# A four-batch retention and low-rank mixer kernel: batches 1 to 3 in natural token order, stored by whole tiles

## The chip, the cores and the metric

The kernel runs on one core of a Trainium2 chip. A time is the device time of one execution in microseconds, given as the median of several executions. Line numbers (L757 and so on) are those of the kernel before.

## What is computed

There are 4 batches, 8 heads, 768 tokens and a head width of 64. The first half is a linear recurrence per head, the second a mixer over tokens and then over channels; everything comes in and goes out as fp32.

```python
# q, k, v: [4, 8, 768, 64]; gamma[h] = 1 - 2**(-5-h)
for t in range(768):
    state = gamma * state + outer(k[:, :, t], v[:, :, t])
    y[:, :, t] = q[:, :, t] @ state / 8
x = y moved to [4, 768, 512]           # heads side by side
h = x.transpose(0, 2, 1) @ U @ V       # over tokens, rank 32: U [768, 32], V [32, 768]
u = x + h.transpose(0, 2, 1)
out = u + relu(u @ w_ch1) @ w_ch2      # over channels, 512 -> 2048 -> 512
```

## The kernel before, in words

**Stages.** The recurrence is done in blocks of tokens: a score matrix inside a block (L505), a causal mask on it (L511, `mask`), the product with v (L527) and, for what came before the block, a running state (L489, L522). Batch 0 has functions of its own (`turn_block`, `score_block`, `mix_block`). For batches 1 to 3, `weave` (L820) interleaves the recurrence of batch b with the channel mixer of batch b-1: the mixer's pieces (`mlp_pieces`, L746) stand in a fixed order, and each step of the recurrence has a written-out place, a share of the pieces' total cost. Each engine works through its own instructions in the order in which they were written down.

**The mixer of a batch.** `up` (L757) makes gT = relu(w1 u): 16 pieces over the first four blocks of 128 tokens (`lo`), 16 over the last two (`hi`), woven as eight `lo`, eight `hi`, and then the rest. The relu is done by ScalarE (L764), for every fourth piece by VectorE (L762), and frees one of four PSUM banks. It reads uT, the transposed u, which for batches 2 and 3 comes from three DMA transposes on SyncE's queue (`lr_turn`, L591); the third holds the last two token blocks and so serves the `hi` pieces. `down` (L805, batch 0) and `down_pairs` (batches 1 to 3) make the second product; `down_pairs` uses a scheme with 7 products in place of 8 (L649, sums in L599). `give` (L670) and `halves` (L710) finish an output tile of 128 tokens and put it on the list `stores`.

**Token order.** q arrives two neighbouring tokens to a partition, each a run of 128 numbers ("(p two)"), so that a descriptor is 512 bytes long. After the transpose, `q_order` (L452) copies the two halves into place: for block x, first the even tokens, then the odd ones ("two m"). Hence x, u and the output tiles have even tokens in partitions 0 to 63 and odd ones in 64 to 127; U and V are brought into that order at the start (`spread_u`, `spread_v`), `mask` is made from `t2` (the same order), and `store` (L603) writes every tile as two DMAs of 64 partitions, one to the even and one to the odd rows.

**Queues.** SyncE issues all loads (`feed_one`, L155), the transposes of k and q of batches 2 and 3 (`turn_dma`, L474), those of u (L591) and most stores (L608). Loads go through a ring of 16 tiles: GpSimd takes one (`prep_keys`, L304 and L306; `prep_w1`, `prep_w2`) and the next load follows. The stores of batch 1 are issued by ScalarE (12 DMAs), those of batches 0, 2 and 3 by SyncE, except one of the last. In the program as built, every DMA takes the next of eight completion semaphores in program order and, before it is issued, waits for the DMA that used it last, so DMA n waits for DMA n-8 whatever queue that is on. GpSimd also makes half of the sums of w2 (L599, `w2_sums`).

Of the kernel before, what the change touches and what calls it, by code (L numbers as in the profile page):

```python
# [13 lines left out]
ALU = mybir.AluOpType  # L14
# [4 lines left out]
def kernel(  # L19
# [63 lines left out]
    def evac(eng, dst, src):  # L83
        if eng == "A":
            nc.scalar.activation(dst, src, AF.Copy)  # L85
        else:
            nc.vector.tensor_copy(out=dst, in_=src)
# [5 lines left out]

    Ub = wts.tile([P, NCK, RK], fp16)
    V4 = wts.tile([P, S], fp16)
    VR = NSC * RK
    Uf = blk.tile([P, NSC, 2, RK], fp32, bufs=1)
    Vf = blk.tile([VR, SC], fp32, bufs=1)  # L100
# [36 lines left out]
    def feed_one(hold=True):  # L137
        if n_fed[0] == len(feed):
            return
        if hold and feed[n_fed[0]][0][:2] == ("k", 3):  # L140
            return
        key, src = feed[n_fed[0]]
        n_fed[0] += 1
        if key[0] == "uv":
            nc.sync.dma_start(
                out=Uf.rearrange("p s two r -> p s (two r)"),
                in_=moe_U.rearrange("(s p two) r -> p s (two r)", p=P, two=2))
            nc.sync.dma_start(
                out=Vf, in_=moe_V.rearrange("r (f t) -> (r f) t", f=NSC))
            return  # L150
        t = rin.tile([P, 512], fp32, tag="in", name=f"in_{n_fed[0]}")
        ready[key] = t
        if key[0] in "qkv":
            t = t.rearrange("p (h d) -> p h d", h=H if len(key) == 3 else 4)
        nc.sync.dma_start(out=t, in_=src)  # L155

# [14 lines left out]
    for b in range(1, B):  # L171
        for sc in range(NSC):
            feed_keys(pair(b, sc)[AHEAD * (b == 1 and sc == 0):])
    for _ in range(RING):
        feed_one()

# [23 lines left out]
    def tables(eng, dims, iota, only_k=False):  # L200

        n = len(dims)
        lg = consts.tile([P, *dims, H], fp32, name=f"lg{n}")
        pos = consts.tile([P, *dims, H], fp32, name=f"pos{n}")
        t = [consts.tile([P, *dims, H], fp32, name=f"g{i}{n}")
             for i in ("kk" if only_k else "qk")[only_k:]]
        nc.gpsimd.iota(pos, base=0, allow_small_or_imprecise_dtypes=True, **iota)
        for h in range(H):
            eng.memset(lg[..., h], gammas_log[h])
        eng.tensor_tensor(pos, pos, lg, op=ALU.mult)  # L210
        nc.scalar.activation(t[-1], pos, AF.Exp, scale=-1.0)
        if only_k:
            return t[0]
        nc.scalar.activation(t[0], pos, AF.Exp)
        eng.tensor_scalar(t[0], t[0], 1.0 / math.sqrt(D), None, op0=ALU.mult)
        return t
# [108 lines left out]
        return u_p  # L325

    def hold_u(u_p):
        evac("A", Ub.rearrange("p (s x) r -> p x s r", x=2),
             u_p[:, :NCK * RK].rearrange("p (x s r) -> p x s r", x=2, s=NSC))

    def spread_v():
        v_p = [bank(t) for t in ("st", "qk")]
        for f in range(NSC):
            nc.tensor.matmul(v_p[f // 2][:, ts(f % 2, SC)], v_sel[:VR, f], Vh,
                             start=(f % 2 == 0), stop=True,
                             skip_group_check=True)
        evac("A", V4[:, :2 * SC], v_p[0])
        evac("A", V4[:, 2 * SC:], v_p[1][:, :SC])

    def prep_w1(mb):  # L340
        for c in range(NCB):
# [109 lines left out]

    def q_order(b, sc, src):  # L452
        t = rmid.tile([P, 2, 4, P], bf16, tag="qO", bufs=2, name=f"qO_{b}_{sc}")
        dst = t.rearrange("p x n (two m) -> p two n x m", two=2)
        src = src.rearrange("p two n (x m) -> p two n x m", x=2)
        for two in range(2):
            evac("A" if b == 1 else "D", dst[:, two], src[:, two])
        live["qO", b, sc] = t
# [82 lines left out]
    def lr_proj(b):  # L541
        p_p = bank("o" if b else "s")
        for j in range(NCK):
            for c in range(NCB):
                nc.tensor.matmul(p_p[ds(RK * c, RK), :P], Ub[:, j],
                                 xs[b][:, j, ts(c, P)], start=(j == 0),
                                 stop=(j == NCK - 1))
        pcs[b] = rmid.tile([P, P], fp16, tag="pc", name=f"pc_{b}")
        evac("D", pcs[b], p_p[:, :P])
# [3 lines left out]
    def lr_grow(b, j0, nj, last="qk"):  # L553
        banks = [bank(t) for t in ("s", "s", "o", last)]
        grown[b] = banks
        for j in range(j0, j0 + nj):
            for c in range(NCB):
                nc.tensor.matmul(banks[c][:, ts(j - j0, P)],
                                 V4[ds(RK * c, RK), ts(j, P)],
                                 pcs[b][ds(RK * c, RK)], start=True, stop=True)  # L560

    def lr_add(b, j0, nj, cs=range(NCB)):
# [40 lines left out]
    def store():  # L603
        if stores:
            eng, dst, src = stores.pop(0)
            dst = dst.rearrange("(p two) c -> two p c", two=2)
            for i in range(2):
                eng.dma_start(out=dst[i], in_=src[ds(HP * i, HP)])  # L608

    def chain(*fs):  # L610
        def f():
# [134 lines left out]
    def mlp_pieces(b):  # L746
# [52 lines left out]
        def down(j, m0):  # L799
            def f():  # L800
                if m0 == 0:
                    hold[j] = bank("mlp")
                ch = hold[j]
                for m in range(m0, m0 + 4):
                    nc.tensor.matmul(ch, gT[:, m, ts(j, P)], w2b[:, m],  # L805
                                     start=(m == 0), stop=(m == NM - 1))
                if m0 == NM - 4:
                    o_sb = outp.tile([P, DM], fp32, tag="o_sb",
                                     name=f"o_{b}_{j}")
                    nc.vector.tensor_tensor(o_sb, ch, us[b][:, j], op=ALU.add)  # L810
                    stores.append((nc.scalar if b else nc.sync,
                                   out[b, ts(j, P)], o_sb))
            return f

        for j in range(NCK):
# [41 lines left out]
    for sc in range(NSC):  # L857
        last = sc + 1 == NSC
        keep_busy(3 if sc else 9, fresh=not last, wide=not sc)
        turn_block("k", sc, "D")  # L860
        keep_busy(0 if sc else 7, wide=True)
        turn_block("q", sc, "AD" if last else "A")
        prep_pair("v", sc, "PD" if last else "PA")
        if sc:
            state_half(sc - 1, 1)
        else:
            keep_busy(4)
        score_block(sc, 0)
        if last:
            prep_uv()  # L870
        else:
            prep_pair("k", sc + 1, "PD")
            prep_block("P", "q", sc + 1, 0)
            keep_busy(0 if sc else 3)
        if sc:
            score_block(sc, 1, "mlp", "DA")
        else:
            score_block(sc, 1)
        if last:
            u_p = spread_u()  # L880
            state_half(sc, 0)
            hold_u(u_p)
            mix_block(sc - 1, "AD")
            continue
        prep_block("D", "q", sc + 1, 1)
        if sc:
            mix_block(sc - 1, "AA")
        keep_busy(4 if sc else 1, fresh=sc > 0)
        state_half(sc, 0)
        if sc == 0:  # L890
            nc.vector.tensor_scalar(mask, t2.rearrange("p two m -> p (two m)"),
                                    srange, None, op0=ALU.is_ge)
    for mb in range(4):
        prep_w1(mb)
    mix_block(NSC - 1, "AD", ("s", "s"))
# [11 lines left out]
    idle_bank[0] = bank("s")  # L907
    for c in range(NCB):
        nc.tensor.matmul(xT[c][:, :LO], pcs[0][ds(RK * c, RK)],
                         V4[ds(RK * c, RK), :LO], start=False, stop=True,  # L910
                         skip_group_check=True)
    for c in range(NCB):
        evac("AD"[c % 2], uTs[0][:, :NLO, c], four(xT[c]))
# [7 lines left out]
    for b in range(1, B + 1):  # L921
# [10 lines left out]
        if b < B:  # L932
            if b == 1:
                at = [0.475, 0.575, 0.63, 0.69, 0.745, 0.8]
                lag = [0.01, 0.035, 0.065]
                for sc in range(NSC):
                    keys = pair(b, sc)
                    c0, c1 = 2 * sc, 2 * sc + 1
                    if sc:
                        tracks.append(([part(prep_keys, b, keys[:AHEAD])],  # L940
                                       at[c0] - 0.1, 1))
                    tracks.append(([part(prep_keys, b, keys[AHEAD:])],
                                   at[c1] - 0.1, 1))
                    for f, d in ((part(turn_pe, "q", b, sc),
                                  at[c0] - (0.035, 0.025, 0.03)[sc]),
                                 (part(turn_pe, "k", b, sc, (0,)), at[c0]),
                                 (part(turn_pe, "k", b, sc, (1,)), at[c1])):
                        tracks.append(([f], d, d))
                for sc in range(NSC):
                    tracks.append(([part(prep_keys, 2, pair(2, sc))],  # L950
                                   at[-1] - 0.05 + 0.03 * sc, 1))
# [83 lines left out]
```

## Time and profile before

| | |
|---|---|
| median of 5 runs | 227.77 us (226.03 to 229.68) |
| the profiled execution | 227.15 us, of which the span shown is 225.3 us |
| granted TensorE clock | 9 of 10 or more in every slice |
| TensorE busy (PE) | 213.2 us, 95% |
| VectorE (DVE), ScalarE (ACT), GpSimd (POOL) busy | 143.6, 89.2 and 92.3 us |
| packets on SyncE's DMA queue | 83776, 36.84 MB |
| stores, SyncE's queue | 32 of 128 KB, 6 of 64 KB, 2 of 32 KB |
| stores, ScalarE's queue | 12 of 128 KB, 2 of 32 KB |

PE, DVE, ACT, POOL are engines; SPq and ACTq are the instruction queues of SyncE and ScalarE, where DMAs are issued. A row of the timeline is: start, duration, engine, line, operation, out<-in, and in brackets how long the engine stood idle before it and what ended that. A row of the groups has busy time, mean ns of one and idle time before them. The chain of waits follows the work that ended last backwards to what released it. The whole profile is of one execution.

### The profile page before, as it was taken

How to read it: one execution, taken by the hardware profiler on the slowest of the kernel's cores; microseconds unless marked ns; L12 is line 12 of the kernel's file. 1: busy time of each engine (PE TensorE's matmuls, PEld its weight loads, DVE VectorE, ACT ScalarE, POOL GpSimd, SP SyncE). 2: the span in 40 equal slices, each digit the busy share in tenths (PEclk: the TensorE clock that was granted, in tenths of full speed). 3: DMA queues.
4: the chain of work that ended last, by engine and by line, in shares of the span. 5: the costliest groups of instructions: out<-in, count | busy, mean ns of one | idle time of the engine just before them, and what ended most of it. 6: DMA issues, size and time to landing. Idle time of an engine off the chain costs nothing.

```text
span 225.3 us, 5543 instructions
## 1 busy us (share of the span) xinstructions
PE 213.2 (95%) x2235; PEld 148.0 (66%) x2235; DVE 143.6 (64%) x294; ACT 89.2 (40%) x187; POOL 92.3 (41%) x129
## 2 busy tenths in 40 slices
PE   7898999999999999899999995999999999999991
PEld 2677844695565455665887852755888847668891
DVE  6488546336585572999896653596967543766541
ACT  3266654474664136576410006667310036550000
POOL 5467878887788789910599400000000000000000
PEclk9999999999999999999999999999999999999999
DMA  6999999999989999999999999000002990000263
GB/s 178 300 293 267 285 370 290 370 319 219 233 179 252 230 245 190 197 206 235 223 219 230 191 249 206 4 0 3 0 3 65 153 203 1 3 1 0 54 146 83
DMA packets 84921, 38.83 MB, mean 172 GB/s; under 512 B 58816, under 2 KB 77984, under 8 KB 84896
## 3 DMA queue, kind: packets, MB, share of 16 engines
q1 hardware_dynamic: 83776, 36.84, 70.0%
q10 hardware_dynamic: 1120, 1.64, 2.6%
q8 instruction: 17, 0.28, 0.6%
q14 instruction: 8, 0.07, 0.1%
HBM read 27.46 MB, written 6.29 MB: 150 GB/s over the span
## 4 chain that ended last, share of the span: by engine, by line
PE 70%; DVE 8%; SPq 8%; DMA 7%; issue 3%; POOL 1%; ACT 0%; ACTq 0%; POOLq 0%; DVEq 0%
PE mlp L757 33%; PE A L649 9%; PE mlp L805 9%; SPq L155 4%; PE C L649 3%; DMA in<-in_q_dram 3%; SPq L591 3%; DMA qT<-qd 3%; PE B L649 2%; DVE gS L599 2%; PE s L505 2%; DVE a L511 2%; PE o L527 2%; DMA uT<-x 1%; PE qk L464 1%
## 5 line engine op out<-in xcount | busy, mean ns | idle before, releaser
L757 PE MATMUL mlp<-uT,w1b 128*128 128x512 f16 (+1 forms) x512 | 88.8, 326 | 3.0 <-ACT gT L764 2.4
L764 ACT ACTIVATE gT<-mlp 128x512 f16<-128x512 f32 (+1 forms) x94 | 45.2, 490 | 65.9 <-PE mlp L757 45.4
L757 PEld LDWEIGHTS <-w1b 128*128 128x128 f16 x512 | 48.4, 98 | 33.9 <-issue 3.4
L762 DVE TENSOR_SCALAR gT<-mlp 128x512 f16<-128x512 f32 (+1 forms) x34 | 18.9, 555 | 30.5 <-PE mlp L757 30.5
L649 PEld LDWEIGHTS <-gT 128*128 128x128 f16 x288 | 27.5, 98 | 3.5
L511 DVE TENSOR_TENSOR a<-s,mask 128x512 bf16<-128x512 f32 x36 | 23.1, 683 | 9.8 <-PE s L505 9.6
L805 PE MATMUL mlp<-w2b,gT 128*128 128x512 f16 x96 | 24.1, 380 | 0.0
L306 POOL TENSOR_TENSOR kd<-in,gk 128x512 bf16<-128x512 f32 x18 | 19.2, 1076 | 5.6 <-DMA in<-in_k_dram 5.5
L649 PEld LDWEIGHTS <-gS 128*128 128x128 f16 x200 | 19.3, 98 | 2.6
L85 ACT ACTIVATE x<-o 128x512 f16<-128x512 f32 x20 | 11.9, 596 | 21.1 <-PE o L527 20.9
L306 POOL TENSOR_TENSOR qd<-in,gq 128x512 bf16<-128x512 f32 x18 | 19.1, 1078 | 1.4 <-DMA in<-in_q_dram 1.4
L649 PE MATMUL A<-w2t,gT 128*128 128x256 f16 x144 | 18.3, 273 | 0.0
L85 ACT ACTIVATE state<-st 64x256 bf16<-64x256 f32 x40 | 15.0, 375 | 5.4 <-PE st L385 3.9
L805 PEld LDWEIGHTS <-gT 128*128 128x128 f16 x96 | 8.2, 98 | 7.5
L304 POOL CAST vd<-in 128x512 bf16<-128x512 f32 x18 | 11.5, 650 | 1.4 <-PE s L505 0.7
L342 POOL CAST w1b<-in 128x512 f16<-128x512 f32 x16 | 9.6, 614 | 2.3 <-DMA in<-in_moe_w_ch_dram 1.8
L348 POOL CAST w2b<-in 128x512 f16<-128x512 f32 x16 | 9.6, 614 | 1.5 <-DMA in<-in_moe_w_ch_dram 1.0
L564 DVE TENSOR_TENSOR x<-s,x 128x256 f16<-128x256 f32 (+1 forms) x16 | 8.1, 551 | 2.1 <-ACT gT L764 1.1
L649 PE MATMUL B<-w2b,gT 128*128 128x256 f16 x72 | 9.4, 273 | 0.0
L649 PE MATMUL A<-w2t,gS 128*128 128x256 f16 x72 | 9.2, 273 | 0.0
L649 PE MATMUL A<-w2b,gT 128*128 128x256 f16 x72 | 9.0, 273 | 0.0
L599 DVE TENSOR_TENSOR gS<-gS,gT 128x768 f16<-128x768 f16 x12 | 8.3, 690 | 0.3
(148 smaller groups left out, 280.6 us busy)
## 6 DMA issues: line engine op xcount, KB each, us to landing
in<-in_moe_w_ch_dram SPq DMA_DIRECT2D x32, 256.0 KB, 5.7
in<-in_k_dram SPq DMA_DIRECT2D x24, 256.0 KB, 5.4
in<-in_q_dram SPq DMA_DIRECT2D x24, 256.0 KB, 5.1
in<-in_v_dram SPq DMA_DIRECT2D x24, 256.0 KB, 5.5
out_dram<-o SPq DMA_DIRECT2D x32, 128.0 KB, 2.4
out_dram<-o ACTq DMA_DIRECT2D x12, 128.0 KB, 4.1
out_dram<-o SPq DMA_DIRECT2D x6, 64.0 KB, 2.1
Uf<-in_moe_U_dram SPq DMA_DIRECT2D x1, 96.0 KB, 6.0
```

The costliest lines, as they stand in the source:

```text
L85: nc.scalar.activation(dst, src, AF.Copy)
L304: nc.gpsimd.tensor_copy(out=t, in_=src)
L306: nc.gpsimd.tensor_tensor(t, src, g, op=ALU.mult)
L342: nc.gpsimd.tensor_copy(out=w1b[:, c, ts(mb, 512)], in_=take("w1", mb, c))
L348: nc.gpsimd.tensor_copy(out=w2b[:, m], in_=take("w2", m))
L511: nc.vector.tensor_tensor(a, four(sp[i]), causal(mask), op=ALU.mult)
L599: return lambda: f(*args, **kw)
L649: nc.tensor.matmul(acc[key, i], lhs[:, m, ts(i, P)], rhs[:, m], start=(fresh and m == 0), stop=(m == NH - 1), skip_group_check=True)
L757: nc.tensor.matmul(g_p[:, :sz], w1b[:, c, ts(m, P)], uTs[b][:, ds(j, nj), c], start=(c == 0), stop=(c == NCB - 1))
L762: nc.vector.tensor_relu(gT[:, m, ds(lo, sz)], g_p[:, :sz])
L764: nc.scalar.activation(gT[:, m, ds(lo, sz)], g_p[:, :sz], AF.Relu)
L805: nc.tensor.matmul(ch, gT[:, m, ts(j, P)], w2b[:, m], start=(m == 0), stop=(m == NM - 1))
```

## The change

`q_order` writes the two halves interleaved ("m two": every second element) and not one after the other, so from there on batches 1 to 3 are in natural token order; batch 0 stays as it was. Batches 1 to 3 therefore have U and V of their own (`Ub[1]`, `V4[1]`): a new step `order_uv` loads U once more through the ring of 16, ahead of batch 2's keys, in runs of 128 bytes, and GpSimd casts it and copies V4 into natural order (two GpSimd instructions, one DMA). It stands at the share `at[-1] - 0.06` of batch 1's weave, just ahead of `prep_keys` for batch 2. `mask` is made from `jmat`. `store` issues one DMA for a tile; batch 0's tiles are put on the list as two halves, as before. So batch 1 has 6 stores on ScalarE's queue in place of 12; batches 2 and 3 have half as many on both queues. Two small tables move to a pool that is released earlier.

```diff
-    Ub = wts.tile([P, NCK, RK], fp16)
-    V4 = wts.tile([P, S], fp16)
+    Ub = [wts.tile([P, NCK, RK], fp16, name=f"Ub{i}") for i in range(2)]
+    V4 = [wts.tile([P, S], fp16, name=f"V4{i}") for i in range(2)]
...
+        if b == 1:
+            feed.append((("u",), moe_U.rearrange("(j p) r -> p j r", p=P)))
...
+    def order_uv():
+        nc.gpsimd.tensor_copy(
+            out=Ub[1], in_=take("u")[:, :NCK * RK].rearrange(
+                "p (j r) -> p j r", j=NCK))
+        feed_one()
+        nc.gpsimd.tensor_copy(
+            out=V4[1].rearrange("p (j t two) -> p j two t", two=2, t=HP),
+            in_=V4[0].rearrange("p (j two t) -> p j two t", two=2, t=HP))
...
     def q_order(b, sc, src):
         t = rmid.tile([P, 2, 4, P], bf16, tag="qO", bufs=2, name=f"qO_{b}_{sc}")
-        dst = t.rearrange("p x n (two m) -> p two n x m", two=2)
+        dst = t.rearrange("p x n (m two) -> p two n x m", two=2)
...
-                nc.tensor.matmul(p_p[ds(RK * c, RK), :P], Ub[:, j],
+                nc.tensor.matmul(p_p[ds(RK * c, RK), :P], Ub[b > 0][:, j],
...
-                                 V4[ds(RK * c, RK), ts(j, P)],
+                                 V4[b > 0][ds(RK * c, RK), ts(j, P)],
...
     def store():
         if stores:
             eng, dst, src = stores.pop(0)
-            dst = dst.rearrange("(p two) c -> two p c", two=2)
-            for i in range(2):
-                eng.dma_start(out=dst[i], in_=src[ds(HP * i, HP)])
+            eng.dma_start(out=dst, in_=src)
...
-                    stores.append((nc.scalar if b else nc.sync,
-                                   out[b, ts(j, P)], o_sb))
+                    dst = out[b, ts(j, P)].rearrange("(p two) c -> two p c",
+                                                     two=2)
+                    for i in range(2):
+                        stores.append((nc.sync, dst[i], o_sb[ds(HP * i, HP)]))
...
-            nc.vector.tensor_scalar(mask, t2.rearrange("p two m -> p (two m)"),
-                                    srange, None, op0=ALU.is_ge)
+            nc.vector.tensor_scalar(mask, jmat, srange, None, op0=ALU.is_ge)
...
+                tracks.append(([order_uv], at[-1] - 0.06, 1))
```

More of the change, by code (lines that the diff above doesn't have):

```diff
@@ L152, in feed_one @@
         ready[key] = t
-        if key[0] in "qkv":
+        if key[0] == "u":
+            t = t[:, :NCK * RK].rearrange("p (j r) -> p j r", j=NCK)
+        elif key[0] in "qkv":
             t = t.rearrange("p (h d) -> p h d", h=H if len(key) == 3 else 4)
@@ L202, in tables @@
         n = len(dims)
-        lg = consts.tile([P, *dims, H], fp32, name=f"lg{n}")
-        pos = consts.tile([P, *dims, H], fp32, name=f"pos{n}")
+        lg = blk.tile([P, *dims, H], fp32, name=f"lg{n}", bufs=1)
+        pos = blk.tile([P, *dims, H], fp32, name=f"pos{n}", bufs=1)
         t = [consts.tile([P, *dims, H], fp32, name=f"g{i}{n}")
@@ L327, in hold_u @@
     def hold_u(u_p):
-        evac("A", Ub.rearrange("p (s x) r -> p x s r", x=2),
+        evac("A", Ub[0].rearrange("p (s x) r -> p x s r", x=2),
              u_p[:, :NCK * RK].rearrange("p (x s r) -> p x s r", x=2, s=NSC))
@@ L336, in spread_v @@
                              skip_group_check=True)
-        evac("A", V4[:, :2 * SC], v_p[0])
-        evac("A", V4[:, 2 * SC:], v_p[1][:, :SC])
+        evac("A", V4[0][:, :2 * SC], v_p[0])
+        evac("A", V4[0][:, 2 * SC:], v_p[1][:, :SC])
+    def order_uv():
[6 more added lines that the diff above has]
+            in_=V4[0].rearrange("p (j two t) -> p j two t", two=2, t=HP))
     def prep_w1(mb):
@@ L909 @@
         nc.tensor.matmul(xT[c][:, :LO], pcs[0][ds(RK * c, RK)],
-                         V4[ds(RK * c, RK), :LO], start=False, stop=True,
+                         V4[0][ds(RK * c, RK), :LO], start=False, stop=True,
                          skip_group_check=True)
```

## The prediction

> **What bounds the kernel now.** I read the engine shares first, then the chain of waits, then the timeline around each place where TensorE (PE) waits.
>
> ```profile
> PE 213.2 (95%) x2235; PEld 148.0 (66%) x2235; DVE 143.6 (64%) x294; ACT 89.2 (40%) x187; POOL 92.3 (41%) x129
> ```
>
> PE is busy for 95% of the span. The change adds and removes no matmul, so only PE's gaps and what follows its last matmul can move. From 28 us on the timeline has five gaps: 0.68 at 92.3, 0.31 at 100.7, 0.28 at 113.9, 2.41 at 135.3 and 0.55 at 180.8; then 4.3 us from PE's last product (about 221.0 with its sum) to the end. The chain of waits goes through the largest gap:
>
> ```profile
> 123.74 1.29 DVE x L564 x2
> ...
> 129.16 1.44 SPq L474
> ...
> 130.69 5.75 DMA qT<-qd
> ...
> 136.47 0.47 ACTq L608
> ...
> 137.06 0.61 ACT gT L764
> ...
> 137.71 1.02 PE mlp L757 x4
> ```
>
> ScalarE's last store of batch 1 waits for a transpose of q (landing 136.45); behind it on ScalarE stand the relus of batch 2's mixer, and behind those PE, for want of a free bank. The timeline there, and at the next gap:
>
> ```profile
> 121.67 15.27 ACTq L608 DMA_DIRECT2D out_dram<-o  x12
> ...
> 136.87 1.68 SPq L591 DMA_TRANSPOSE uT<-x  x1
> 137.06 1.57 ACT L764 ACTIVATE gT<-mlp 128x512 f16<-128x512 f32 x3 [18.43 <-DMA out_dram<-o]
> 137.71 1.02 PE L757 MATMUL mlp<-uT,w1b 128*128 128x512 f16 x4 [2.41 <-ACT gT L764]
> ...
> 142.05 1.47 PE L757 MATMUL mlp<-uT,w1b 128*128 128x256 f16 x12
> ```
>
> ```profile
> 171.69 3.71 SPq L608 DMA_DIRECT2D out_dram<-o  x6
> ...
> 175.56 3.91 SPq L591 DMA_TRANSPOSE uT<-x  x2
> ...
> 181.37 8.81 PE L757 MATMUL mlp<-uT,w1b 128*128 128x512 f16 x48 [0.55 <-DMA uT<-x]
> ```
>
> Six stores stand ahead of batch 3's transposes of u on SyncE, and PE waits 0.55 us for the second.
>
> **The change, part by part.**
>
> *Place A, ScalarE's stores of batch 1 (12 to 6).* The wait of each store follows from the count of semaphores: transfer n waits for n-8. Before, the last two waited for kT and qT of batch 3's middle block. Counted again with half the stores, the six wait for: a load, a load, a load, qT of batch 3's first block, the first uT, and a store issued at 125.4. These land at about 120.2, 121.1, 122.8, 129.1 (issued 122.5, 6.5 to landing), 130.6 and 130.4. The last store now waits for its own data: VectorE's row L670 at 131.34 plus 0.42 is 131.76. An issue costs 0.55 us here, so ScalarE is free at about 132.4, when PE's first bank of batch 2 (131.46 plus 0.98) is ready, in place of 137.06. The 2.41 us go.
>
> What is late next: the `hi` pieces. PE starts them at 142.05, 4.34 us after the gap's end at 137.71; without the gap at 139.64. They read the third uT, issued at 136.87 and 3.7 us from issue to landing: 140.6. Left as it is, it puts back 0.95 us. Two things move it. (a) SyncE issues kT, qT and that uT back to back at 1.93, 1.98 and 1.68 us while ScalarE's stores run; where no store runs (91.3, 178.2, 183.4) one takes 1.3. With those stores done by 134.5 it could be up to 1.3 us sooner, 139.3. (b) `order_uv` adds a load to the same stream (below), up to 0.7 us later, 141.3. The DMA engines' share is 0.94 from 131 to 142, and the stores keep their bytes. [...] I take 140.3, nearer to the rule: **A gives 1.75 us** (0.75 to 2.41).
>
> *Place B, batch 2's stores (6 issues ahead of uT to 3).* Their last data come from L670 at 173.44 plus 0.42, 173.86; one issue of 0.55 brings SyncE to uT at 174.5 in place of 175.56. Both transposes (3.91) and 3.1 to land give 180.3 or sooner, and PE is ready at 180.82. **B gives 0.55 us** (0.4 to 0.55). The third uT comes earlier too; PE needs it only after eight pieces.
>
> *Place C, the end.*
>
> ```profile
> 211.55 11.41 SPq L608 DMA_DIRECT2D out_dram<-o  x16
> ...
> 220.74 0.29 DVE L710 TENSOR_TENSOR o<-B,db 128x128 f32<-128x128 f32 x1 [0.16 <-PE B L705]
> ```
>
> The last sum ends at 221.03. SyncE is then still issuing second halves: its two DMAs for this piece start at 221.8 and 222.4, and the latter lands 1.9 later, at 224.3. After: one store of o_3_5 from 220.3 to 220.85, then the last from 221.05, landing 2.1 later (the median of stores of 64 KB) at 223.15. **C gives 1.2 us** (0.9 to 1.35).
>
> *The copies of q_order on VectorE* (6 in batch 2, 6 in batch 3) now write every second element. The groups by form:
>
> ```profile
> L87 DVE COPY qO<-qT 128x512 bf16<-128x512 bf16 x12 | 4.8, 445 | 0.0
> L272 DVE CAST v<-in 128x512 bf16<-128x512 f32 x1 | 0.4, 427 | 0.0
> L762 DVE TENSOR_SCALAR gT<-mlp 128x512 f16<-128x512 f32 x17 | 11.7, 690 | 21.5 <-PE mlp L757 21.5
> ```
>
> A free copy takes 284 to 288 ns (minimum and median in the tile's view; the first two, held by something, 1.24 us at most). [...] The first two pairs lie on the chain (89.96 to 101); the third and batch 3's have slack (PE has no gap from 137.7 to 180.8). Cost 0.55 (0.3 to 2.4).
>
> *order_uv.* GpSimd: casts of 192 and 512 elements take 342 and 614 ns, so U's is 0.34 and V's, 768 elements, 0.83 by the same slope (up to 1.3 if its stride costs): 1.2 us. The load: 768 runs of 128 bytes. By bytes (98 of 262 KB) it is 0.37, by runs (768 of 1024) 0.75 of a load of k, which follow each other at about 1.35 us: 0.5 to 1.0, I take 0.7. PE needs Ub[1] at 75.96 and V4[1] at 77.39; the load takes the place of one that landed at 67.4, so both are there by 69. Everything behind it on SyncE and GpSimd slides: batch 2's loads, its six transposes, batch 0's stores (from 92.66), batch 3's loads (from 100.3), and the w2 sums (87.0). The first reader to notice is VectorE:
>
> ```profile
> 85.13 1.25 SPq L474 DMA_TRANSPOSE qT<-qd  x1
> ...
> 90.57 2.39 DVE L87 COPY qO<-qT 128x512 bf16<-128x512 bf16 x2
> ...
> 93.01 0.40 PE L505 MATMUL s<-qO,kT 64*128 64x128 bf16 x8 [0.68 <-DVE qO L87]
> ```
>
> That qT lands 4.4 after its issue, at 89.5, and is wanted at 90.6: a cover of 1.0 against 0.7. If the cover is gone, relus and sums queue behind the copy on VectorE and PE waits for them; 0 to 0.3. The w2 sums are wanted only at 112.5, 16 us after they end. Batch 3's slide meets a SyncE pause of 0.8 us at 124.3 and ends there, except in the transfers (term b of A).
>
> *The sum.* Batch 2's costs (0.55, with qT 0.7) come before A. They make PE reach `hi` at 140.2 to 140.35, when the third uT is there at 140.3 anyway: they cost nothing more, their cover being that wait. ScalarE's own q_order copies (594 ns, batch 1) have no row with such a stride; at double they add 1.2 us a pair, ScalarE is about 55% busy there and PE has no gap; a gain is excluded, none is my value, 0.6 the upper end. The mask, the tables and natural order as such cost nothing: same instructions, sizes and order. So 1.75 + 0.55 + 1.2 = 3.5: the span goes from 225.3 to 221.8, the profiled execution from 227.15 to 223.65. The median shown is 0.62 above that execution: **224.3 us**.
>
> **The rivals.**
> - *Nothing takes the place of the stall.* The third uT comes by 139.6 and batch 2's costs hide: 2.41 + 0.55 + 1.2 = 4.2, 223.6. For it: the 1.3 us issues where no store runs. Against it: a DMA share near 1.
> - *The transfers take it back,* or the change does not free ScalarE: uT at 141.3 or later, or another late semaphore. A gives 0.3: 2.0 in all, 225.8. For it: same bytes and one more load. Against it: the waits as counted.
> - *Slower: batch 2's stage on VectorE becomes the bound.* From 90 to 118 VectorE is busy for over 90%. While GpSimd makes the w2 sums (87.04 to 96.58) VectorE's copies take 1.24 for 0.29 and its sums 1.06 to 1.42 for 0.55. If GpSimd's sums slide by 3 us, into the second pair of copies and the sums after 97, that is two copies at 0.95 and six sums at 0.5 to 0.87, some 6 us. B and C return 1.75 and A at most 2.41, so it decides from 4.2 us of PE delay on; at 6, 229.5. Against it: the slide is worked out at 1.2, not 3.
>
> **How the numbers follow.** The forecast has 0.55, the full gain 0.15, the transfers 0.20, the slower one 0.10. One per cent is 2.3 us, about what a measurement of this kernel can tell from no change. Below 225.5: most of the forecast (0.49), the full gain (0.14), a little of the third (0.04): 0.67. Above 230.0: 0.06. Between: 0.27. The likeliest case alone has 223.5 to 225.7 by the ends of A, B and C; with the runs' scatter and the third rival, 222.8 to 226.6 holds 8 in 10.
>
> **What would show it.** Right: ScalarE's relus of batch 2 start within 1 us of PE's first piece; PE's wait of 2.41 is gone, and a wait for uT of 0 to 1 us stands ahead of `hi`; none for uT at batch 3's start; last store issued within 0.1 us of the last sum; copies of q_order at 0.43; GpSimd's two new instructions 1.2 together. Wrong: ScalarE still waiting for a transpose, copies at 0.69, VectorE waiting for qT at 91, or PE gaps from 90 to 118 above 2 us.

## The result, and the profile after

| | before | changed |
|---|---|---|
| median of all runs | 227.77 us (223.96 to 230.49, 80 runs) | 225.83 us (223.78 to 229.22, 43 runs) |
| ratio, first measurement | | 0.9965 (95%: 0.9944 to 0.9985) |
| ratio, again on another chip | | 0.9927 (0.9892 to 0.9962) |
| the profiled execution, its span | 227.15, 225.3 us | 225.9, 224.1 us |

The ratios leave out each kernel's slowest runs (over 1.5% above its fastest), which are more frequent in the kernel before, so that the medians lie further apart, 1.9 us, than the ratios say. By the two ratios the change is worth 0.8 and 1.7 us, where 3.5 were forecast. The time itself lies in the range given; the forecast gain is two to four times the one measured.

These are the lines that answer to those of before. First the busy time of the engines:

```profile
PE 214.6 (96%) x2235; PEld 148.1 (66%) x2235; DVE 143.5 (64%) x294; ACT 90.3 (40%) x187; POOL 93.9 (42%) x131
```

The two added GpSimd instructions are there (131 for 129). The chain of waits through batch 2's first mixer pieces (start, duration, what):

```profile
128.00 1.23 SPq L604
...
129.33 5.38 DMA uT<-x
...
134.85 2.75 PE mlp L768 x12
...
139.89 3.25 DMA uT<-x
...
143.18 1.48 PE mlp L768 x12
```

ScalarE's stores have gone from the chain, and transposes of u stand in their place. The timeline at the same place:

```profile
124.50 10.54 ACTq L619 DMA_DIRECT2D out_dram<-o  x6
...
134.85 2.75 PE L768 MATMUL mlp<-uT,w1b 128*128 128x512 f16 x12 [0.49 <-DMA uT<-x]
...
135.99 0.60 ACT L775 ACTIVATE gT<-mlp 128x512 f16<-128x512 f32 x1 [14.53 <-DMA out_dram<-o]
...
139.89 1.28 SPq L604 DMA_TRANSPOSE uT<-x  x1
...
143.18 1.48 PE L768 MATMUL mlp<-uT,w1b 128*128 128x256 f16 x12 [0.15 <-DMA uT<-x]
```

ScalarE's first relu starts 1.14 us after TensorE's first product (before: 5.6). The wait of 2.41 us is gone, but TensorE waits 0.49 and 0.15 for the second and third uT, and it comes to this place at 134.85, not at 131.46. The timeline at batch 3's start and at the end:

```profile
172.83 2.85 SPq L619 DMA_DIRECT2D out_dram<-o  x3
175.86 3.61 SPq L604 DMA_TRANSPOSE uT<-x  x2
...
212.09 9.85 SPq L619 DMA_DIRECT2D out_dram<-o  x8
...
221.28 0.29 DVE L721 TENSOR_TENSOR o<-B,db 128x128 f32<-128x128 f32 x1 [0.15 <-PE B L716]
```

At batch 3's start (181 before) TensorE has no wait any more, and from its last product to the end pass 2.9 us in place of 4.6. The groups by form, and VectorE's copies in the tile's view (minimum, median, maximum):

```profile
L87 DVE COPY qO<-qT 128x512 bf16<-128x512 bf16 x12 | 5.9, 550 | 0.0
...
L85 ACT ACTIVATE qO<-qk 128x512 bf16<-128x512 bf16 x6 | 4.0, 740 | 2.1 <-PE qk L477 2.1
...
L349 POOL COPY V<-V 128x768 f16<-128x768 f16 x1 | 1.0, 1049 | 0.0
...
L345 POOL CAST Ub<-in 128x192 f16<-128x192 f32 x1 | 0.3, 347 | 0.0
```

```profile
L87 DVE COPY qO<-qT x12: 447/450/1393, 92.7 to 157.1; 128x512 bf16<-128x512 bf16 x12
```

A free strided copy on VectorE takes 447 to 450 ns (284 to 288 before), on ScalarE 740 (594).

**Where it went, by the two traces.** The matmuls are the same 2235 in the same order, so the start of one in both traces gives TensorE's lateness, after minus before, at a time of the trace before. It is 0.7 us at 52, 2.10 from 70 to 89, 2.83 at 109 and still 2.83 at 131. Across place A it falls to 1.14, at batch 3's start to 0.54, and the end comes 1.2 sooner. So A gave 1.69, B 0.60 and C 1.75, in all 4.0 where 3.5 were forecast, and 2.83 had been lost ahead of A, where the forecast let 0.7 be lost and hidden. (How much of the 2.83 is the change's, and how much is the scatter of single executions, the experiments tell.)

### The profile page after: what moved, and what is told of

It is laid out like the page before. It is cut to its first block, busy times and chain, and to the rows that moved or that the text cites. A ratio compares the mean times of both kernels' runs of the same rounds, so it can differ in the third digit from the quotient of the medians.

```text
span 224.1 us, 5520 instructions
## 1 busy us (share of the span) xinstructions
PE 214.6 (96%) x2235; PEld 148.1 (66%) x2235; DVE 143.5 (64%) x294; ACT 90.3 (40%) x187; POOL 93.9 (42%) x131
## 4 chain that ended last, share of the span: by engine, by line
PE 64%; DMA 17%; DVE 10%; POOL 3%; ACT 2%; issue 2%; SPq 1%; DVEq 0%; ACTq 0%
PE mlp L768 24%; PE A L660 11%; DMA in<-in_moe_w_ch_dram 7%; PE mlp L816 6%; DMA in<-in_k_dram 6%; PE C L660 5%; DMA uT<-x 4%; PE B L660 3%; PE mlp L193 3%; DVE gS L612 2%; DVE a L524 2%; PE s L518 2%; PE o L540 2%; POOL qd L310 1%; ACT qO L85 1%
## 5 line engine op out<-in xcount | busy, mean ns | idle before, releaser
L540 PE MATMUL o<-vd,a 128*128 128x64 bf16 x144 | 7.7, 193 | 1.1 <-DVE a L524 1.1
## 6 DMA issues: line engine op xcount, KB each, us to landing
out_dram<-o SPq DMA_DIRECT2D x15, 128.0 KB, 2.4
```

The source lines that it names most:

```text
L540: nc.tensor.matmul(o_p[:, ts(h, D)], a[i][:, h // 2], vb[:, h], start=(ci == 0 and h == 0), stop=True, skip_group_check=True)
```

## The experiments

Two theories. L: the gain is all in the stores, and the new order loses part of it ahead of place A. S: the order costs nothing; a profile shows one execution, and the late start is its scatter. Ratios are to the kernel before on the same chip.

**The change again, and its stores alone.** `after_again` is unchanged. `stores_only` and `stores_again` are the kernel before with

```diff
-            dst = dst.rearrange("(p two) c -> two p c", two=2)
-            for i in range(2):
-                eng.dma_start(out=dst[i], in_=src[ds(HP * i, HP)])
+            eng.dma_start(out=dst, in_=src)
```

and batch 0 stored in halves, as in the changed kernel.

> The changed kernel once more, as the yardstick for the three beside it. Its profile showed the gains at the three places of the stores at 2.3, 0.6 and 1.7 us, and TensorE already 1.6 us later than before at 58 us, ahead of everything that the change does. Theory 1 (the losses lie in the added work: copies and order_uv): 0.991 to 0.997 of before, TensorE again 1.5 us late at 58 us or not, but 1 to 2 us lost between 58 and 132 us. Theory 2 (the late loads of the first 58 us are scatter of one execution, so the profile alone is unlucky): at 58 us within 0.5 us of before, and the span 222.5 to 223.5. Theory 3 (the moved tables and the new tiles made the first 58 us slower for good): 1.6 us late at 58 us again.

> The kernel before with the whole-tile stores alone: token order, copies, U and V stay as they were, so the rows of batches 1 to 3 leave in the even-odd order (the outputs are permuted). Theory 1: all three gains and none of the losses, 2.3 + 0.6 + 1.7 = 4.6 us less than before, ratio 0.980. Theory 2: the same as theory 1. Theory 3: 0.980 as well, since the tables did not move, and 3 us or more under the changed kernel. Rival (the gains of the stores overlap with the third transpose of u, so they are worth only 2 to 3 us even alone): ratio 0.988 or more.

> The kernel before with whole-tile stores alone, a second time and on another chip, since six runs were too few (its rows land in another order inside a tile). Theory L: the 3.5 us of the prediction's steps A, B and C are all here, ratio 0.981 to 0.988, and the order gives 1 to 2.5 of them back in the changed kernel. Theory S: the stores alone give no more than the whole change, ratio 0.990 to 0.997.

Measured: `after_again` 225.5 us, 0.9927; `stores_only` 224.08, 0.9837 (0.9771 to 0.9902); `stores_again` 224.19, 0.9854 (0.9792 to 0.9917). The stores alone are worth 3.3 to 3.7 us: the sum of A, B and C as forecast. Their two profiles, single executions of 226.74 and 225.75 us, have B at 0.6 and C at 1.7 as well, but A at only 0.3 and 0.0, as TensorE waits there too: 1.56 us ahead of the first and 0.44 ahead of the `hi` pieces in the one, 0.29 and 2.05 in the other; so the size of A varies from one execution to the next.

**The order alone.** `halves` is the changed kernel with `store` writing two halves of 64 rows again:

```diff
-            eng.dma_start(out=dst, in_=src)
+            for i in range(0, src.shape[0], HP):
+                eng.dma_start(out=dst[ds(i, HP)], in_=src[ds(i, HP)])
```

> The changed kernel with its stores alone undone: each output tile leaves again in two halves of 64 rows (natural order, strided q copies and the second U and V stay). So it shows what the order costs by itself. Theory L (the order costs time ahead of place A: the strided copies, and GpSimd's and the transfer stream's work for the second U and V, which together make batch 2's keys and VectorE late): 1.0 to 2.5 us slower than the kernel before, ratio 1.004 to 1.011, TensorE at 131 us some 1.5 to 3 us later than in the profiles of the kernel before. Theory S (the order costs nothing; the late start of the profiles is the scatter of single executions): ratio 0.998 to 1.002.

Measured: 228.68 us, 1.0088 (1.0045 to 1.0131), 2.0 us slower than the kernel before. The two parts add up: 0.985 times 1.009 is 0.994, between the two measurements of the whole change. Theory S falls: the order costs 1.0 to 3.0 us.

**How far one profile can be trusted.** `before_p1` and `before_p2` are the kernel before, profiled again.

> The unchanged kernel, profiled once more. Theory T2 (the late loads ahead of 58 us are the scatter of single executions, and the first profile of this kernel happened to lack them): in at least one of this run and its twin TensorE shows the gap of 0.5 to 0.75 us at 58 us and reaches its 900th product (75 to 78 us) 1.5 to 2.7 us later than in the first profile, as four of the five profiles of the changed kernels do; and the wait for ScalarE at 135 us is then smaller than 2.41 by about as much, 0 to 1.2, since it ends at a transfer's landing. Rival T3 (something in the change itself slows the first 58 us): both runs lie within 0.5 us of the first profile up to 88 us, with no gap at 58 and a wait of 2 us or more at 135.

> The twin of the run before: the unchanged kernel, profiled once more. T2 and T3 expect what they expect there; together the two runs and the first profile give three values for the wait at 135 us. If that wait is 2.2 to 2.6 us in all three, the size of place A in the prediction was not the profile's scatter.

Measured: 227.8 and 225.6 us. The wait at place A is 2.24 and 1.70 (first profile 2.41), so its size was a little high, not a freak. TensorE is 0.68 and 0.83 late at 77 us; the gaps of 0.71 that the changed kernel's profiles have at 58 are not there. Neither theory of that stretch held: the lateness at 77 us is -0.6 to 0.8 in the seven profiles of kernels whose stores of batches 0 and 2 are as before, 0.3 to 2.7 in the twelve others but `one_issue`, and 2.7 in `stores_only`, whose program is the same as the kernel before up to 92 us. So it isn't the order's alone, and its cause stays open. But `before_p1` showed something that was not looked for. Its windows (busy time of TensorE, its weight loads, VectorE, ScalarE and GpSimd, then the granted clock, DMA share, GB/s):

```profile
132.00:136.00 4.00, 2.70 (x16) 1.25 (x15) 1.50 (x5) 0.00 (x0) 0.00 (x0) 1.00 1.23 204
136.00:140.00 4.00, 3.06 (x15) 1.08 (x15) 0.80 (x2) 2.80 (x6) 0.00 (x0) 0.64 0.93 233
140.00:144.00 4.00, 4.00 (x34) 2.49 (x33) 1.18 (x2) 2.34 (x5) 0.00 (x0) 0.93 0.02 4
```

After the wait of 2.24 us the clock is 0.64 for four us and 0.93 for four more, 1.7 us of full clock lost (4 x 0.36 + 4 x 0.07).

**The steps A and C by themselves.** In the kernel before, whole tiles for batch 1 alone (`scalar_whole`, `scalar_again`), batch 3 alone (`end_whole`), both (`scalar_end`):

```diff
-            eng, dst, src = stores.pop(0)
+            eng, dst, src, b = stores.pop(0)
+            if b in (1, 3):
+                eng.dma_start(out=dst, in_=src)
+                return
```

> The kernel before with another part alone: batch 1's outputs, ScalarE's stores, leave by whole tiles (6 issues in place of 12; their rows land in another order inside a tile). By the prediction's step A, 1.75 us faster, ratio 0.992. By the rival that the wait at 135 us is mostly a product of one execution, in which TensorE came early and the transposes did not, TensorE waits for transposes of u or q there instead: 0 to 0.8 us faster, ratio 0.9965 to 1.0, with a wait for uT of 0.4 to 1.6 us ahead of the first pieces of batch 2's mixer or ahead of the hi pieces.

> The kernel before with ScalarE's stores of batch 1 alone by whole tiles, a second time, on another chip: six runs gave 1.007 (1.000 to 1.013) although TensorE's wait for ScalarE was gone in the profile. If step A is worth what the prediction says, 1.75 us, ratio 0.990 to 0.995; if A alone brings nothing because the transposes behind it are as late, 0.998 to 1.004.

> The kernel before with one part of the change alone: batch 3's outputs, the last eleven stores, leave by whole tiles (their rows land in another order inside a tile). The step C of the prediction says the last store then lands 1.2 us sooner after TensorE's last product; the five profiles with whole-tile stores show 1.7 (2.8 us from the last product to the end, in place of 4.5). So 1.2 to 1.7 us faster than the kernel before, ratio 0.9925 to 0.995, and nothing changed ahead of 205 us. If transfers and not issues set the end, the ratio is 1.0 and the tail stays at 4.5.

> The kernel before with batch 1's and batch 3's stores by whole tiles and batch 2's in halves: steps A and C without B. If the steps add up, 1.75 plus 1.2 to 1.7: ratio 0.985 to 0.988. If A alone and C alone bring as little as their six runs each said (1.007 and 1.001), 0.998 to 1.005, and the gain of the whole-tile stores, 1.5 per cent, would have to hang on B or on having all three.

Measured: `scalar_whole` 227.48 us, 1.0069 (1.0004 to 1.0134); `scalar_again` 226.11, 0.9958 (0.9923 to 0.9994); `end_whole` 226.88, 1.0009 (0.9939 to 1.0079); `scalar_end` 224.58, 0.9873 (0.9819 to 0.9927). A and C together are 2.9 us, the 2.95 of the forecast. Alone neither is settled: the two runs of A contradict each other, and `end_whole` shows the shorter tail in its timeline

```profile
211.56 9.85 SPq L607 DMA_DIRECT2D out_dram<-o  x8
...
220.75 0.29 DVE L713 TENSOR_TENSOR o<-B,db 128x128 f32<-128x128 f32 x1 [0.15 <-PE B L708]
```

(2.9 us from the last product to the end) and yet no gain: in five of its six runs the mean granted clock is 0.992 or less, which is 1.8 us of 226; its wait at A is still there (2.32 us, then 0.67 and 0.91 of the clock).

**What in the order costs: the copies, or the second U and V.** From the changed kernel, `plain_copies` writes blocks as before, `no_order_uv` and `no_uv_again` leave the second U and V out (batches 1 to 3 use batch 0's, which don't fit their order), `no_uv_plain` does both:

```diff
-        dst = t.rearrange("p x n (m two) -> p two n x m", two=2)
+        dst = t.rearrange("p x n (two m) -> p two n x m", two=2)
...
-                tracks.append(([order_uv], at[-1] - 0.06, 1))
```

> The changed kernel with q_order's copies writing runs of 64 as before (so q of batches 1 to 3 is in the even-odd order while U, V, mask and rows are natural; part of the computation is changed). Copies at 0.29 on VectorE in place of 0.45 and 0.59 on ScalarE in place of 0.74. Theory 1: TensorE's waits for ScalarE's copies (0.13, 0.18 and part of 0.7 us at 58 to 69) and 0.2 to 0.4 at 93 to 104 go: 0.5 to 0.9 us under the changed kernel. If order_uv is the whole loss: no change.

> The changed kernel without order_uv: no second load of U, no cast and no copy on GpSimd; batches 1 to 3 use batch 0's U and V, whose order does not fit theirs (part of the computation is changed). Theory 1 puts 0.5 (wait for the second transpose of u) plus some of the 0.7 lost from 93 to 104 us on it: 0.5 to 1.2 us under the changed kernel. If the copies are the whole loss: no change. Theory 3: no change at 58 us.

> The changed kernel without the second U and V and without their load (batches 1 to 3 use batch 0's U and V: their part of rank 16 is that of permuted rows), a second time, since six runs were too few. If the load and the work for the second U and V cost about 1 us, ratio 0.985 to 0.990; if they cost nothing, as the prediction has it, 0.992 to 0.997.

> The same, with the copies of q writing blocks as before in place of every second element (so the outputs are in the old order inside a tile, in the wrong rows, and the mask does not fit): what stays of the changed kernel is its whole-tile stores, its tables in another pool and its mask from another tile. If copies and second U and V are all of the order's price, ratio 0.982 to 0.988, as with the stores alone; if the strided copies cost nothing, as fast as the run beside it.

Measured: `plain_copies` 225.69 us, 0.9924 (0.9894 to 0.9954); `no_order_uv` 224.88, 0.9879 (0.9811 to 0.9947); `no_uv_again` 224.95, 0.9920 (0.9890 to 0.9950); `no_uv_plain` 225.22, 0.9906 (0.9877 to 0.9935). The times don't tell these four from each other, nor clearly from the changed kernel at 0.9965 and 0.9927; only `no_uv_plain` lies below the first of these two intervals. Three further kernels split the second U and V: `load_only` keeps the load without the work, `uv_scalar` gives the work to ScalarE, and `one_load` loads U once, in natural order.

```diff
-        nc.gpsimd.tensor_copy(
-            out=Ub[1], in_=take("u")[:, :NCK * RK].rearrange(
-                "p (j r) -> p j r", j=NCK))
+        evac("A", Ub[1], take("u")[:, :NCK * RK].rearrange(
+            "p (j r) -> p j r", j=NCK))
```

> The changed kernel with the second load of U kept in the ring of loads but no second U and V made from it (batches 1 to 3 use batch 0's U and V: their part of rank 16 is that of permuted rows). Against the version without both, 0.988: if the load costs, 0.992 to 0.996; if GpSimd's 1.4 us cost, 0.985 to 0.990.

> The changed kernel with the second U and V made by ScalarE in place of GpSimd; the load of U stays where it is in the stream of loads. If GpSimd's 1.4 us are what costs (batch 2's q, k and v and the w2 sums behind them slide), this is as fast as the version without the second U and V: ratio 0.985 to 0.990, and the w2 sums start before 88.5 us. If the load is what costs, it stays at the changed kernel's 0.992 to 0.997; if ScalarE has no room at 68 us, it is slower than that.

> A version meant to beat both: the changed kernel, but U is loaded once, in natural order, at the start in place of the old order; two products with a permuted identity give batch 0's order of it, and VectorE copies V into natural order near 45 us, where it is busy a third of the time. So the ring of loads is as it was before, and GpSimd has nothing more to do. If the second load of U (its 0.7 us in the stream of loads) is what makes the order dear, ratio 0.983 to 0.990, the w2 sums start before 88.5 us less TensorE's own lateness, and TensorE's gaps of 0.40 and 0.46 us near 100 and 102 us go. If the strided copies are what makes it dear, ratio 0.992 to 0.996.

Measured: `load_only` 226.32 us, 0.9931 (0.9900 to 0.9962); `uv_scalar` 225.50, 0.9953 (0.9921 to 0.9986); `one_load` 226.49, 0.9946 (0.9907 to 0.9985), so it doesn't beat the changed kernel. `load_only` and `uv_scalar` lie where their expectations put the load, and not GpSimd's work, as the price, but so does `no_uv_again`, which has neither. Where the times can't, the traces tell what happens in batch 2's first stage. `stores_again`, timeline:

```profile
96.32 1.15 POOL L599 TENSOR_TENSOR w2t<-w2b,w2t 128x512 f16<-128x512 f16 x1
...
97.80 0.55 DVE L599 TENSOR_TENSOR gT<-gT 128x768 f16<-128x768 f16 x1
...
101.87 0.29 PE L527 MATMUL o<-vd,a 128*128 128x64 bf16 x4 [0.31 <-DVE a L511]
```

and `halves`, which has the second U and V:

```profile
96.89 1.47 POOL L612 TENSOR_TENSOR w2t<-w2b,w2t 128x512 f16<-128x512 f16 x1
...
97.27 1.50 DVE L612 TENSOR_TENSOR gT<-gT 128x768 f16<-128x768 f16 x1
...
99.16 1.02 PE L769 MATMUL mlp<-uT,w1b 128*128 128x512 f16 x4 [0.40 <-DVE gT L774]
...
101.96 0.29 PE L540 MATMUL o<-vd,a 128*128 128x64 bf16 x4 [0.46 <-DVE a L524]
```

In `halves` GpSimd's last w2 sum falls on one more of VectorE's sums, which takes 1.50 in place of 0.55, and TensorE waits 0.40 and 0.46. The loss in this stage goes with how long after TensorE has reached its 991st matmul (88.7 us in the first profile) GpSimd ends these sums. In the twelve profiles of kernels with neither a second U and V nor a load for them, that is 5.9 to 7.9 us, and TensorE's lateness changes by -1.4 to +0.1 from there to 109 us (the earlier the sums, the more it gains; the first profile of before is among the latest, 7.9 and 0.0). In the five with both it is 7.8 to 9.5, and 0.2 to 1.1 are lost. `load_only`, where GpSimd does nothing for U and V, has 9.3 and loses 1.2, so in this one execution the load went with late sums without that work: GpSimd's conversions of batch 2's k, q and v wait for loads (0.42 to 0.69 us at a time from 75 to 89 us in the first profile of the changed kernel), and the sums stand behind them. It is not the only way: `one_load`, without it, has 8.8 and loses 0.7, for a reason that was not found. In all nineteen the loss grows with the lateness of the sums.

**The gain without the order.** `one_issue` is the kernel before, with one transfer for a tile whose rows are permuted by the address pattern:

```diff
-            for i in range(2):
-                eng.dma_start(out=dst[i], in_=src[ds(HP * i, HP)])
+            eng.dma_start(out=dst, in_=src)
```

> The second version meant to beat both: the kernel before, with the order inside a tile left as it is; only the store changes, one transfer for a whole tile, whose address pattern in main memory takes the even rows for the first 64 partitions and the odd ones for the rest. Its outputs are in their right places. If the stores alone carry the gain and the order only costs, ratio 0.980 to 0.990 (0.984 and 0.985 with whole-tile stores in the wrong rows); if such a pattern is issued as slowly as two halves (0.47 to 0.59 us each), ratio 0.998 to 1.002.

Measured: 317.9 us, 1.404 (1.398 to 1.411). Its timeline (six stores of batch 0) and a window of the same stretch:

```profile
91.91 19.97 SPq L607 DMA_DIRECT2D out_dram<-o  x6
```

```profile
108.00:116.00 8.00, 8.00 (x100) 6.91 (x98) 6.65 (x15) 2.14 (x5) 0.19 (x1) 1.00 0.14 53
```

By the completion counts in the trace the six stores finish one every 5.1 us, from 100.0 to 125.6 us (at the window's 53 GB/s a store of 256 KB would take 4.9), where the changed kernel's whole tiles on SyncE land 2.0 us after issue (median). Meanwhile the DMA share is 0.14 of the 16 engines' time, as much as two of them busy throughout (0.125), and everything behind on SyncE is late. The outer dimension of this pattern is 2 in main memory and 128 in SBUF; a whole tile in natural order has 128 in both. How the pattern sets the share was not shown. No version tried here beats the changed kernel with every output row in its place.

## Why the prediction was wrong, point by point

*Place A, 1.75 us: right in size.* 1.69 by the first traces, by the mechanism given: ScalarE free, the rest put back by a wait for uT. Single executions scatter (1.6 in `after_again`, 0.3 and 0.0 with the stores alone), so the timed sums carry this more than the one trace does. The third uT was to land at 140.3; it landed at 143.1, and TensorE came as much later. Counted from TensorE's place that is 0.2 us sooner than before (140.55), so half the issues with the same bytes moved that landing by 0.2 us. No run shows a rule for where that uT lands: the 140.3, and the 1.75 with it, was the author's estimate between 139.3 and 141.3; measured are 143.1, or 140.3 counted from TensorE's place. Not foreseen: a wait of 0.49 for the second uT. Its pair is issued as late as TensorE (128.0 for 125.2), but lands 6.7 us after that in place of 6.1.

*Place B, 0.55: right* (0.60 by the traces; not timed alone). *Place C, 1.2: right, and too low*: 1.75; the last store landed 1.6 us after its issue, not 2.1. A and C together were timed at 2.9 for 2.95 (interval 1.7 to 4.1), all stores at 3.3 to 3.7 for 3.5.

*The copies of q_order on VectorE: right.* 450 ns, near the row of 427 and not that of 690. No row of before has a copy that writes every second element, so the 0.55 for batch 2 was the author's estimate (four copies at 427 less 287 ns); measured are 0.16 us more a copy (450 less 287). Between the profiles without second U and V, strided and plain copies differ by 0.2 us of TensorE's lateness in that stage at most. *GpSimd's two instructions: nearly right*, 1.40 us for 1.2, as the copy of V takes 1.05 and not 0.83. *The copies on ScalarE, valued at 0, cost about 0.3*: they take 740 ns, and TensorE has two new gaps of 0.13 and 0.18 us at 61 and 69 in every profile of a kernel that has them, and in none of the two with plain copies.

*The step that failed is the one in the sum: "Batch 2's costs (0.55, with qT 0.7) come before A. They make PE reach `hi` at 140.2 to 140.35, when the third uT is there at 140.3 anyway: they cost nothing more, their cover being that wait."* The order costs 2.0 us (1.0 to 3.0), as `halves` shows, and nothing covers it. The cover was taken to be a landing at a fixed time. But what ends that wait starts from TensorE's own progress. GpSimd begins batch 3's conversions only after `gate`, a copy of one column of gT (L791) that waits for one of the last relus of batch 1, and the first two transposes of u wait for VectorE's x, whose last sum ends 0.15 us ahead of them (at 125.02 before, at 127.85 after). Before, and after:

```profile
109.22 0.42 DVE L762 TENSOR_SCALAR gT<-mlp 128x256 f16<-128x256 f32 x1 [0.59 <-PE mlp L757]
109.71 0.19 POOL L599 COPY gate<-gT 128x1 f16<-128x1 f16 x1 [13.13 <-DVE gT L762]
...
125.17 3.90 SPq L591 DMA_TRANSPOSE uT<-x  x2
```

```profile
112.05 0.42 DVE L773 TENSOR_SCALAR gT<-mlp 128x256 f16<-128x256 f32 x1 [0.57 <-PE mlp L768]
112.54 0.19 POOL L612 COPY gate<-gT 128x1 f16<-128x1 f16 x1 [12.93 <-DMA in<-in_k_dram]
...
128.00 3.97 SPq L604 DMA_TRANSPOSE uT<-x  x2
```

Relu, `gate` and uT all come 2.83 us later, which is TensorE's lateness. (The second `gate` names a load in its bracket, but it starts 0.06 us after the relu's end, as in every profile.) GpSimd's last conversion of batch 3 ends 2.83 later as well, at 129.34 for 126.51, and behind these conversions stand the transposes of k and q that SyncE issues ahead of the third uT. In all twenty profiles `gate` starts as late as TensorE is at that point, to 0.01 us, whatever had made it late. So the wait for uT moves along with TensorE: counted from TensorE's place at 131 us, the third uT lands at 140.3 and 140.4 in the two profiles of the changed kernel, which is the 140.3 of the forecast (139.4 to 142.3 in the nineteen profiles other than `one_issue`, as the transfers scatter). The pause of SyncE at 124.3, in which batch 3's slide was to end, is the wait for x, and moves along in the same way.

Of the 2.0, about 0.7 are the second U and V in batch 2's first stage (mean loss there 0.7 in the five profiles with them and their load, 0.0 in the three of the changed kernel without) and 0.3 ScalarE's copies, both by traces. The rest has no cause yet: `no_uv_plain`, which keeps neither copies nor second U and V, is at 0.9906, and the stores alone are at 0.9837 and 0.9854; the intervals touch. What is left between them, two tables in another pool, the mask and two more tiles, wasn't tried by itself. The traces give a hint of the place: from the 991st matmul to 109 us the nine profiles in the old order gain 0.7 us in mean (0.0 to 1.4), while the three of the changed kernel without second U and V gain nothing.

*The rival on the slower side had the right mechanism and too high a threshold.* It let GpSimd's sums slide by 3 us before anything happened. They slid by about 1.1 against TensorE, and that cost 0.7: the loss grows with the slide. The first profile of before hid this, as it has these sums nearly as late as any without the change; in the other two profiles of that kernel they come earlier, and TensorE gains 1.4 us in that stage.

*Left out altogether: the clock.* The wait at A was followed by a lower clock in some executions (1.7 us of full clock in `before_p1`), so removing it was worth more than its length there.

## What to carry to other kernels

A cost is covered by a wait only if what ends the wait does not depend on what is late. Before calling it free, follow what ends the wait back from releaser to releaser: here from the transfer over SyncE and GpSimd to a copy that waits for TensorE's own work. Undo the gain and the price separately: two runs, the stores alone and the order alone, told in numbers what no comparison of two traces could, since single executions of one kernel differ here by 1.4 us at the same relu (88.76 and 87.34 us in the profiles of `stores_only` and `stores_again`). Merging two transfers paid here where the merged pattern had 128 rows as its outer dimension (0.9837 and 0.9854 with the stores alone), and cost 40% where that dimension was 2 (1.404 in `one_issue`), so price a merge by the pattern and not by the count of issues alone.

## What the runs showed of the hardware

A lower clock followed some of TensorE's waits of little more than 2 us here. Of the five profiles with a wait of 2.24 us or more at place A or at the `hi` pieces (`one_issue` apart), three show the clock at 0.57 to 0.67 over the four us that follow; of those with less, none does. In the timed runs beside the experiments the kernel before has a mean granted clock under 0.9935 in 71 of 184, and these are 1.9 to 2.7 us slower than the others; the changed kernel has it in 8 of 66. That wait is not the whole account of it: `no_uv_plain`, whose profile waits 0.79 us at most there, has it in 7 of 22. Nor does its length decide alone: the clock fell to 0.64 after 2.24 us in one execution (`before_p1`), and stayed at 1.00 after 2.41 in another (the first profile of before).

Some of VectorE's copies and sums of 16-bit tiles took longer while GpSimd made its sums: a pair of copies took 2.39 us beside them at 90.6 and 0.49 after them at 99.2 (first profile of before), but 0.49 beside them at 91.25 in `before_p1`; a sum of 0.55 took up to 1.50 (`halves`).
